# Chunked delta-rule attention before a Fourier-mixing MLP: chunks of 64 tokens instead of 128, triangular blocks inverted on VectorE instead of TensorE

## The chip, the cores and the metric

One core of one Trainium2 chip. The metric is the time of one execution in device microseconds (us); the median of several runs counts.

## The reference, cut to what matters

```python
B, H, S, D = 4, 8, 768, 48              # fp32 throughout
k_n = k / (norm(k) + 1e-6)
for t in range(S):                      # per batch and head, state is D x D
    y[t]  = q[t] @ state
    v_old = state.T @ k_n[t]
    state = state + beta[t] * outer(k_n[t], v[t] - v_old)
x   = y as (B, S, H*D = 384)
u   = x + real(fft(fft(x, axis=seq), axis=channel))
un  = (u - mean(u)) / sqrt(var(u) + 1e-6)
out = u + relu(un @ w_ch1) @ w_ch2      # 384 -> 1536 -> 384
```

## The kernel before, in words

The recurrence is done in chunks of C = 128 tokens, one chunk on the 128 partitions, all 8 heads side by side: 4 batches x 6 chunks = 24 steps. `load` (L132) brings a chunk of k, v and q with three DMAs on SP's queue (192 KB each, rows of 192 bytes), two steps ahead. `pre` (L239) does what needs no state: norms of k (L247 to L253), 12 transposes on TensorE (tile `pt`, L267, copied out by ScalarE, L268), the products k k' and k q' (tile `pg`, L281), and the inverse of each head's four 32 x 32 diagonal blocks. That inverse is five rounds of doubling (L306 to L336); a round is 32 small matmuls into `px` and 32 or 64 into `pn`, each on 32 x 32 of the array. The four blocks of a head lie on the four partition groups of 32, so four neighbours in the instruction stream use four different row groups and four different column groups of the array, and all write one PSUM tile of 2 KB a partition. VectorE masks `px` into `Y` (L314), ScalarE copies `pn` into `Tn` (L330, L333).

`seq` (L339) carries the state: subtract k times state (`pk`, L350), solve the four blocks of 32 rows in turn (`pa`, `pu`, L355 to L367), then the state's increment `pS` (L373) and the output `py` (L377, L379), which becomes a row block of `x` (L387).

`post` (L392) takes a finished batch: sums and differences for the real DFT (L402, L403 on POOL, L406 to L413 on VectorE), DFT along the sequence (`pf`) and along the channels (`pb`, L445) with the additions into x and the norm statistics (L451 to L459), then for each of three groups of 256 tokens the normalised rows are transposed (`ptr`), 72 matmuls make `ph` (1536 hidden channels, relu on VectorE and ScalarE in turn, L486, L488) and 48 make `po`, which is added to x and stored. The weights come as 64-bit floats and are turned into fp32 by VectorE and POOL (`weights`, L183): six pieces of 1.5 MB with ten VectorE instructions each, while batch 0's attention runs.

Each fp32 matmul shows as two MATMUL and two LDWEIGHTS records in the profile; a transpose shows as one.

The order of work is written by generators: in step n the loop at L516 advances `seq(n)`, `pre(n+1)` and a side generator (`weights` in batch 0, `post(b-1)` afterwards) in turn; the tile framework then orders instructions on each engine's queue, by and large in that order but moving ready ones ahead. Each engine works off its queue in order. The last `post` runs alone at the end.

Of the kernel before, what the change touches and what calls it, by code (L numbers as in the profile page):

```python
# [9 lines left out]
F32 = mybir.dt.float32  # L10
# [6 lines left out]
C = 128  # L17
W = 32
LEVELS = (1, 2, 4, 8, 16)


def _consts(S, DM):

    p = np.arange(128)
    c = np.arange(W)
    r = p % W
    ident = np.eye(128)
    su = (p[None, :] > p[:, None]).astype(np.float64)
    bd = su * (p[None, :] // W == p[:, None] // W)
    grp = (p[:, None] // W == np.arange(128 // W)[None, :]).astype(np.float64)  # L30
    eye_c = (r[:, None] == c[None, :]).astype(np.float64)
    lev = []
    for n in LEVELS:
        off = ((r[:, None] // n) % 2 == 1) & (c[None, :] // n == r[:, None] // n - 1)
        lev.append(eye_c - off)
    pack = np.concatenate([ident, su, bd, grp, eye_c] + lev, axis=1)
# [27 lines left out]
def kernel(  # L64
# [14 lines left out]
    NC = S // C  # L79
    NP = H // 2  # L80
    NG = 128 // W
# [14 lines left out]
    io = ctx.enter_context(tc.tile_pool(name="io", bufs=2))  # L96
# [3 lines left out]
    def ps_pre(shape, name):  # L100
        return ps.tile(shape, F32, tag="pre", bufs=3, name=name)

    def ps_seq(shape, name):
        return ps.tile(shape, F32, tag="seq", bufs=2, name=name)

    def ps_post(shape, name):
        return ps.tile(shape, F32, tag="post", bufs=3, name=name)
# [9 lines left out]
    NKQ = 2  # L117
    kqs = []
    for i in range(NKQ):
        t = const.tile([128, 3, H, 64], F32, name=f"kq{i}")  # L120
        nc.gpsimd.memset(t, 0.0)
        kqs.append(t)
    states = []
    for i in range(2):
        t = const.tile([128, NP, 2, D], F32, name=f"state{i}")
        nc.gpsimd.memset(t, 0.0)
        states.append(t)

    steps = [(b, c) for b in range(B) for c in range(NC)]
    loaded = {}  # L130

    def load(n):  # L132
        b, c = steps[n]
        kq = kqs[n % NKQ]
        K4 = io.tile([128, H, D], F32, tag="K4", name="K4")
        V4 = io.tile([128, H, D], F32, tag="V4", name="V4")
        rows = slice(c * C, (c + 1) * C)
        nc.sync.dma_start(out=K4, in_=k[b, :, rows, :].rearrange("h p d -> p h d"))
        nc.sync.dma_start(out=kq[:, 2, :, 0:D], in_=q[b, :, rows, :].rearrange("h p d -> p h d"))
        nc.sync.dma_start(out=V4, in_=v[b, :, rows, :].rearrange("h p d -> p h d"))  # L140
        loaded[n] = (K4, V4)

    pack = const.tile([128, 3 * 128 + NG + W * (1 + len(LEVELS))], F32, name="pack")
    nc.scalar.dma_start(out=pack, in_=cn["pack"].ap())
    bt = const.tile([NBH, S], F32, name="bt")
    nc.scalar.dma_start(out=bt, in_=beta.rearrange("b h s -> (b h) s"))
    load(0)

    ident = pack[:, 0:128]
    m_su = pack[:, 128:256]  # L150
    m_bd = pack[:, 256:384]
    o = 3 * 128
    m_grp = pack[:, o:o + NG]
    eye_c = pack[:, o + NG:o + NG + W]
    m_lev = [pack[:, o + NG + W * (i + 1):o + NG + W * (i + 2)] for i in range(len(LEVELS))]

# [9 lines left out]

    ident_b = const.tile([128, 128], BF16, name="ident_b")
    nc.vector.tensor_copy(ident_b, ident)
    eye_b = const.tile([128, H, W], BF16, name="eye_b")
    nc.vector.tensor_copy(eye_b, eye_c[:, None, :].broadcast_to([128, H, W]))  # L170
    half_p = const.tile([128, H], F32, name="half_p")
    nc.gpsimd.memset(half_p, 0.5)
    half_n = const.tile([128, GT], F32, name="half_n")
    nc.gpsimd.memset(half_n, -0.5)


    psb = ps_pre([128, NC, NBH], "psb")
    for c in range(NC):
        tr(psb[:, c, :], bt[:, c * C:(c + 1) * C], c == 0)
    bcol = const.tile([128, NC, B, H], F32, name="bcol")  # L180
    nc.vector.tensor_copy(bcol.rearrange("p c b h -> p c (b h)"), psb)
# [54 lines left out]
    ready = {}  # L236
    xs = {}

    def pre(n):  # L239

        b, c = steps[n]
        kq = kqs[n % NKQ]
        K4, V4 = loaded.pop(n)
        bc = bcol[:, c, b]

        Ksq = wk.tile([128, H, D], F32, tag="Ksq", name="Ksq")
        nc.gpsimd.tensor_tensor(Ksq, K4, K4, op=ALU.mult)  # L247
        nrm = wk.tile([128, H], F32, tag="nrm", bufs=2, name="nrm")
        nc.vector.tensor_reduce(nrm, Ksq, axis=AX.X, op=ALU.add)
        nc.gpsimd.tensor_tensor(nrm, nrm, half_p, op=ALU.pow)  # L250
        nc.vector.tensor_scalar(nrm, nrm, 1e-6, None, op0=ALU.add)
        nc.vector.reciprocal(nrm, nrm)
        nc.vector.tensor_tensor(kq[:, 0, :, 0:D], K4, nrm[:, :, None].broadcast_to([128, H, D]),  # L253
                                op=ALU.mult)
        nc.gpsimd.tensor_tensor(kq[:, 1, :, 0:D], kq[:, 0, :, 0:D],  # L255
                                bc[:, :, None].broadcast_to([128, H, D]), op=ALU.mult)
        Vb = wk.tile([128, H, D], F32, tag="Vb", bufs=2, name="Vb")
        nc.gpsimd.tensor_tensor(Vb, V4, bc[:, :, None].broadcast_to([128, H, D]), op=ALU.mult)
        yield

        K1T = wk.tile([128, NP, 128], F32, tag="K1T", name="K1T")
        KQT = wk.tile([128, 2, NP, 128], F32, tag="KQT", bufs=2, name="KQT")
        for a, dst in ((2, KQT[:, 1]), (0, K1T), (1, KQT[:, 0])):
            pt = ps_pre([128, NP, 128], "pt")
            src = kq[:, a].rearrange("p h d -> p (h d)")
            for j in range(NP):
                tr(pt[:, j, :], src[:, 128 * j:128 * j + 128], j == 0)  # L267
            nc.scalar.activation(dst, pt, ACT.Copy)  # L268
            yield


        AT = wk.tile([128, H, 128], F32, tag="AT", bufs=2, name="AT")
        LQ = wk.tile([128, H, 128], F32, tag="LQ", bufs=2, name="LQ")
        Abd = wk.tile([128, H, 128], F32, tag="Abd", name="Abd")
        hv = "p (j e) t -> p e j t"
        for a in range(2):
            pgs = [ps_pre([128, NP, 128], f"pg{e}") for e in range(2)]
            for j in range(NP):
                for e in range(2):
                    pr = slice(64 * e, 64 * e + D)  # L280
                    mm(pgs[e][:, j, :], K1T[pr, j, :], KQT[pr, a, j, :], j == 0)  # L281
            for e in range(2):
                pg = pgs[e]
                if a == 0:
                    nc.vector.tensor_tensor(Abd.rearrange(hv, e=2)[:, e], pg,
                                            m_bd[:, None, :].broadcast_to([128, NP, 128]),
                                            op=ALU.mult)
                    nc.scalar.activation(AT.rearrange(hv, e=2)[:, e], pg, ACT.Copy)
                else:
                    nc.vector.tensor_tensor(LQ.rearrange(hv, e=2)[:, e], pg,  # L290
                                            m_su[:, None, :].broadcast_to([128, NP, 128]),
                                            op=ALU.mult)
            yield
# [3 lines left out]


        def blocks(o, lhsT, rhs):
            for h in range(H):  # L300
                for g in range(NG):
                    rw = slice(W * g, W * g + W)
                    mm(o[rw, h, :], lhsT(h, g, rw), rhs(h, g, rw), False)

        T = TT = None
        for i in range(len(LEVELS)):  # L306
            last = i == len(LEVELS) - 1
            px = ps_pre([128, H, W], "px")
            mm(px, ident_b, eye_b, True, False)
            blocks(px, lambda h, g, rw: Abd[rw, h, rw],  # L310
                   (lambda h, g, rw: eye_c[rw]) if T is None else
                   (lambda h, g, rw: T[rw, h, :]))
            Y = wk.tile([128, H, W], F32, tag="Y", bufs=2, name="Y")
            nc.vector.tensor_tensor(Y, px, m_lev[i][:, None, :].broadcast_to([128, H, W]),  # L314
                                    op=ALU.mult)
            yield
            pn = ps_pre([128, 2, H, W], "pn")
            first = [True] * NG
            for a in ((1, 0) if i > 0 and not last else (0,)):
                for h in range(H):  # L320
                    for g in range(NG):
                        rw = slice(W * g, W * g + W)
                        left, right = (TT, Y) if a else (Y, TT)
                        r = eye_c[rw] if right is None else right[rw, h, :]
                        mm(pn[rw, a, h, :], left[rw, h, :], r, first[g])
                        first[g] = False
                yield
# [237 lines left out]
```

## Time and profile before

| what | value |
|---|---|
| median of 3 runs (lowest to highest) | 1342.58 us (1340.2 to 1362.03) |
| the profiled execution's own time | 1334.15 us |
| its span, first to last instruction | 1332.4 us |
| TensorE busy (matmul records) | 1179.3 us, 26758 matmul records |
| VectorE / ScalarE / POOL busy | 411.6 / 252.9 / 171.5 us |

PE is TensorE's matmul row, PEld its weight loads, DVE VectorE, ACT ScalarE, POOL GpSimd, SP the engine whose queue issues most DMAs. A row of the timeline merges neighbouring records of the same kind: its length goes from the first start to the last end. Records of pipelined matmuls overlap, so the pace of a row of n matmuls is its length less one matmul's own duration, divided by n - 1. The granted clock is given as a share of 2.4 GHz, so 0.50 is 1.2 GHz; the clock's own record begins 249 us into the span, and the views show 1.00 before that where nothing was recorded.

### The profile page before, as it was taken

The numbers are of one execution on the slowest core, as the hardware profiler recorded it, in microseconds if no ns is written. First come the engines' busy times: TensorE is split into PE (matmuls) and PEld (weight loads), VectorE is DVE, ScalarE is ACT, GpSimd is POOL, SyncE is SP. The second block draws the span as 40 slices with busy tenths as digits, with TensorE's granted clock in tenths as the row PEclk, the third lists the DMA queues.
The fourth block names the chain that finished last, engine by engine and source line by source line (L and its number), as shares of the span: only waits on it lengthen the run. The fifth ranks groups of instructions, "written<-read, shape, count | busy, mean of one in ns | idle before, by whom it ended". The sixth has DMA issues, their size and how long they took to land. (4 is left out here: it accounts for less than half of the span.)

```text
span 1332.4 us, 55673 instructions
## 1 busy us (share of the span) xinstructions
PE 1179.3 (89%) x26758; PEld 929.8 (70%) x26758; DVE 411.6 (31%) x843; ACT 252.9 (19%) x529; POOL 171.5 (13%) x160
## 2 busy tenths in 40 slices
PE   3688798897899999999889999989989998997998
PEld 2576686786777677676777676766866775766776
DVE  3756721222162132231252222322441221314111
ACT  1111011011132112111321221211321220212000
POOL 4422310120020010120021011110111000001000
PEclk9999999756699899999999999899999999997999
DMA  8321000000010000100010010010100000000000
GB/s 211 104 67 56 15 15 14 16 20 15 3 27 15 21 21 14 33 15 20 10 28 15 20 21 18 22 21 15 21 15 15 14 3 9 8 8 6 12 12 13
DMA packets 81156, 33.60 MB, mean 25 GB/s; under 512 B 75426, under 2 KB 78595, under 8 KB 80547
## 3 DMA queue, kind: packets, MB, share of 16 engines
q1 hardware_dynamic: 80352, 28.32, 8.6%
q8 instruction: 209, 3.42, 1.1%
q10 hardware_dynamic: 578, 1.73, 0.4%
q14 instruction: 17, 0.13, 0.0%
HBM read 25.32 MB, written 4.72 MB: 23 GB/s over the span
## 5 line engine op out<-in xcount | busy, mean ns | idle before, releaser
L110 PE MATMUL ph<-unT,w 128*128 128x256 f32 x864 | 223.0, 397 | 4.8 <-issue 2.9
L110 PE MATMUL po<-w,hT 128*128 128x384 f32 x576 | 208.1, 502 | 0.0
L110 PEld LDWEIGHTS ph<-unT,w 128*128 128x128 f32 x864 | 157.0, 194 | 25.9 <-ACT unT L477 2.8
L110 PEld LDWEIGHTS po<-w,hT 128*128 128x128 f32 x576 | 103.8, 191 | 58.1
L314 DVE TENSOR_TENSOR Y<-px,pack 128x256 f32<-128x256 f32 x120 | 50.6, 422 | 271.6 <-PE px L110 271.5
L110 PE MATMUL pn<-Tn,Y 32*32 32x32 f32 x6144 | 87.4, 206 | 38.1 <-issue 34.1
L110 PEld LDWEIGHTS pn<-Tn,Y 32*32 32x32 f32 x6144 | 74.5, 117 | 56.1 <-issue 46.4
L110 PEld LDWEIGHTS px<-Tn,Abd 32*32 32x32 f32 x4608 | 55.1, 117 | 67.8 <-issue 40.0
L333 ACT ACTIVATE Tn<-pn 128x512 f32<-128x512 f32 x72 | 43.0, 597 | 306.4 <-PE pn L110 306.4
L110 PE MATMUL px<-Tn,Abd 32*32 32x32 f32 x4608 | 66.6, 206 | 36.5 <-issue 28.1
L110 PE MATMUL pg<-KQT,K1T 48*128 48x128 f32 x768 | 89.6, 334 | 2.4 <-ACT KQT L268 2.1
L110 PEld LDWEIGHTS pu<-R,Tn 32*32 32x32 f32 x1280 | 70.1, 119 | 26.6 <-issue 18.6
L110 PE MATMUL pn<-Y,Tn 32*32 32x32 f32 x4608 | 62.6, 205 | 27.5 <-DVE Y L314 24.0
L110 PEld LDWEIGHTS pn<-Y,Tn 32*32 32x32 f32 x4608 | 53.2, 117 | 47.7 <-DVE Y L314 25.7
L361 DVE TENSOR_TENSOR R<-R,pa 32x384 f32<-32x384 f32 x60 | 33.2, 553 | 165.9 <-PE pa L110 165.8
L110 PE MATMUL pu<-R,Tn 32*32 32x48 f32 x1280 | 82.0, 221 | 0.8 <-issue 0.8
L366 ACT ACTIVATE U<-pu 32x384 f32<-32x384 f32 x96 | 46.3, 482 | 187.7 <-PE pu L110 187.3
L110 PEld LDWEIGHTS pg<-KQT,K1T 48*128 48x128 f32 x768 | 73.5, 226 | 10.2 <-ACT KQT L268 3.3
L110 PEld LDWEIGHTS pa<-U,AT 64*32 64x32 f32 (+2 forms) x1152 | 63.3, 122 | 24.4 <-issue 19.8
L255 POOL TENSOR_TENSOR kq<-kq,bcol 128x384 f32<-128x384 f32 x24 | 21.9, 914 | 448.2 <-DVE kq L253 412.0
L110 PE MATMUL pa<-U,AT 64*32 64x48 f32 (+2 forms) x1152 | 74.1, 224 | 0.0
L113 PE MATMUL pt<-pack,kq 128*128 128x128 f32 x288 | 57.9, 335 | 17.6 <-DVE kq L253 9.0
(98 smaller groups left out, 1300.8 us busy)
## 6 DMA issues: line engine op xcount, KB each, us to landing
w<-in_moe_w_ch_dram SPq DMA_DIRECT2D x6, 1536.0 KB, 8.0
K<-in_k_dram SPq DMA_DIRECT2D x24, 192.0 KB, 2.8
V<-in_v_dram SPq DMA_DIRECT2D x24, 192.0 KB, 2.8
kq<-in_q_dram SPq DMA_DIRECT2D x24, 192.0 KB, 2.9
out_dram<-x SPq DMA_DIRECT2D x24, 192.0 KB, 1.9
evt<-k_even ACTq DMA_DIRECT2D x1, 579.0 KB, 6.0
odt<-k_odd ACTq DMA_DIRECT2D x1, 576.0 KB, 7.3
pack<-k_pack ACTq DMA_DIRECT2D x1, 290.0 KB, 3.2
```

The lines of the kernel that those rows point to most:

```text
L110: nc.tensor.matmul(o, lhsT=lhsT, rhs=rhs, start=start, stop=stop, skip_group_check=True)
L113: nc.tensor.matmul(o, lhsT=src, rhs=ident[0:src.shape[0], 0:src.shape[0]], is_transpose=True, start=start, stop=True, skip_group_check=True)
L255: nc.gpsimd.tensor_tensor(kq[:, 1, :, 0:D], kq[:, 0, :, 0:D], bc[:, :, None].broadcast_to([128, H, D]), op=ALU.mult)
L314: nc.vector.tensor_tensor(Y, px, m_lev[i][:, None, :].broadcast_to([128, H, W]), op=ALU.mult)
L333: nc.scalar.activation(Tn, pn, ACT.Copy)
L361: nc.vector.tensor_tensor(R[rw], R[rw], pa[rw], op=ALU.subtract)
L366: nc.scalar.activation(U[rw], pu[rw], ACT.Copy)
```

## The change

What is computed stays. The attention part is written anew; `weights` and the Fourier and MLP code stay, cut into two generators (`fourier`, `mlp`).

- Chunks of C = 64 tokens. A load still covers L = 128 tokens (two chunks). Heads 0 to 3 lie on partitions 0 to 63, heads 4 to 7 on 64 to 127. So there are 24 loads and 48 chunk steps.
- Work that needs no state runs a load or more ahead: `pre_a(g)` (4 transposes of k, the 32 x 32 and 32 x 64 blocks of k k' on array tiles of 64 x 32), `invert(r)` for a round of RL = 4 loads, `pre_b(g)`.
- `invert` puts one 32 x 32 block on each (partition, column) place: two DVE transposes turn the 128 x 1024 tile so that each partition holds one whole block, the norms of k are taken from the blocks' diagonals (ScalarE Sqrt and two Newton steps on VectorE), and forward substitution is 31 steps of one multiply and one add on VectorE over (31-j)(j+1) elements a partition, j = 0 to 30. POOL zeroes the result tile.
- `pre_b` transposes q, joins the two 32-blocks of a 64-chunk (`px`, `py`), masks k q' (`LQ`, VectorE), and multiplies the inverse M by K and by V (`WT`, `U0`) on 64 x 64 tiles of the array.
- `step(g, c)` is then: 8 matmuls `pw` (WT times state), one VectorE subtraction, 8 matmuls `pk`, one VectorE addition into the new state; after the second chunk 32 matmuls and a ScalarE and a VectorE instruction make the output rows of x.
- PSUM: pairs of banks (`pair`, 2 buffers), single ones (`one`, 2), and `post` with 2 buffers where there were 3.
- k, q and v come with four DMAs of 48 KB each per load instead of one of 192 KB, k up to seven loads ahead. beta comes with 32 small DMAs per round of four loads on POOL's queue, where it was one DMA and six transposes at the start.
- The loop: `pre_a` of four loads, `invert(0)` and `pre_b(0)` stand ahead of it. In step n it advances `step`, then parts of `pre_a`, `invert` or `pre_b`, then the side generator (`weights` in batch 0, `mlp(b-1)` afterwards, four pieces a step, nine pieces kept back). After a batch's last step `fourier(b)` runs beside the pieces kept back.

```diff
-C = 128
+C = 64
+L = 128
 W = 32
-LEVELS = (1, 2, 4, 8, 16)
+RL = 4
+RING = 7
...
+    def fetch(dst, src, g):
+        b, n = divmod(g, NL)
+        for hh in range(2):
+            for c in range(2):
+                t0 = n * L + c * C
+                nc.sync.dma_start(out=dst[hh * C:hh * C + C, c],
+                                  in_=src[b, 4 * hh:4 * hh + 4, t0:t0 + C, :].rearrange(
+                                      "j t d -> t j d"))
...
+    def pre_a(g):
+        K = Ks[g % RING]
...
+        for i in range(4):
+            c, jj = divmod(i, 2)
+            tr(pt[:, 128 * i:128 * i + 128],
+               K[:, c, 2 * jj:2 * jj + 2, :].rearrange("p j d -> p (j d)"), i == 0)
+        nc.scalar.activation(KT.rearrange("p c j t -> p (c j t)"), pt, ACT.Copy)
+        yield
...
+        for i in range(4):
+            c, jj = divmod(i, 2)
+            for q4 in range(4):
+                for jp in range(2):
...
+                    mm(pg[q4 * W:q4 * W + W, jp, C * i:C * i + C],
+                       KT[lo[jp], c, jj, t0 + blk * W:t0 + blk * W + W], rhs, i == 0)
...
+    def invert(r):
...
+        nc.gpsimd.memset(M, 0.0)
+        nc.vector.transpose(A, G.rearrange("p m s -> p s m"))
+        yield
...
+        nc.scalar.activation(nrm, diag, ACT.Sqrt)
...
+        nc.vector.scalar_tensor_tensor(A, A, -1.0, bn[:, :, None].broadcast_to([128, W, W]),
+                                       op0=ALU.mult, op1=ALU.mult)
...
+        for j in range(W - 1):
+            n = W - 1 - j
...
+            nc.vector.tensor_tensor(t, A[:, j + 1:W, j:j + 1].broadcast_to([128, n, j + 1]),
+                                    M[:, j:j + 1, 0:j + 1].broadcast_to([128, n, j + 1]),
+                                    op=ALU.mult)
+            nc.vector.tensor_tensor(M[:, j + 1:W, 0:j + 1], M[:, j + 1:W, 0:j + 1], t, op=ALU.add)
+            yield
+
+        nc.vector.transpose(A.rearrange("p m t -> p t m"), M)
+        nc.vector.transpose(G.rearrange("p m s -> p s m"), M.rearrange("p t s -> p s t"))
...
+    def pre_b(g):
...
+        for c in range(2):
+            for j in range(4):
+                for hh in range(2):
+                    mt = MT[full[hh], 4 * c + j].rearrange("p b t -> p (b t)")
+                    jj, jp = divmod(j, 2)
+                    o = (2 * c + jj) * C
+                    mm(pw[full[jp], hh, o:o + C], K[full[hh], c, j, :], mt, c == 0 and jj == 0)
+                    o = (4 * c + j) * D
+                    mm(pu[full[hh], o:o + D], mt, V[full[hh], c, j, :], c == 0 and j == 0)
...
+    def step(g, c):
...
+            pw = ps_pair()
+            for jj in range(2):
+                for hh in range(2):
+                    for jp in range(2):
+                        mm(pw[full[hh], jp, D * jj:D * jj + D], WT[lo[jp], hh, c, jj, :],
+                           s0[lo[jp], hh, jj, :], jj == 0)
+            nc.vector.tensor_tensor(
+                U.rearrange("p (jj jp) e -> p jp jj e", jp=2),
+                U.rearrange("p (jj jp) e -> p jp jj e", jp=2),
+                pw[:, :, 0:2 * D].rearrange("p a (j e) -> p a j e", e=D), op=ALU.subtract)
+            yield
...
+    for g in range(RL):
+        drain(pre_a(g))
...
+    drain(invert(0))
+    load_qv(1)
+    drain(pre_b(0))
     side = weights()
...
+    for n in range(2 * NLT):
...
+        live = [(step(g, c), 1)]
...
+            if ri in (0, 1, 2):
+                live.append((pre_a(nxt + ri), 1))
+            elif ri == 3:
+                live.append((pre_a(nxt + 3), 1))
+                inv = invert(r + 1)
+            elif ri < 7:
+                live.append((part(inv, 12), 3))
...
+            want = (PIECES - KEEP) * (i + 1) // (2 * NL)
+            live.append((part(side, want - done), 2))
...
+        run(live)
+        if i == 2 * NL - 1:
+            if b == 0:
+                drain(side)
+            f = fourier(b)
+            run([(f, 1)] + ([(side, 1)] if b > 0 else []))
+            side, done = mlp(b), 0
+    drain(side)
```

## Rows read from the trace of the kernel before

**Rows 1.** The page: busy time of each engine.

```profile
PE 1179.3 (89%) x26758; PEld 929.8 (70%) x26758; DVE 411.6 (31%) x843; ACT 252.9 (19%) x529; POOL 171.5 (13%) x160
```

**Rows 2.** Stages: length; PE, PEld, DVE, ACT, POOL busy (count); clock; DMA share, GB/s.

```profile
0.00:60.00 60.00, 25.04 (x859) 20.68 (x863) 34.21 (x45) 6.44 (x10) 23.74 (x23) 1.00 0.54 147
60.00:244.00 184.00, 157.15 (x3495) 136.71 (x3491) 82.53 (x110) 29.39 (x57) 39.28 (x19) 1.00 0.15 41
...
885.00:1204.00 319.00, 295.27 (x7136) 224.03 (x7136) 82.16 (x188) 66.46 (x140) 20.62 (x24) 0.98 0.05 13
```

**Rows 3.** Timeline, last `post`: start us, length us, engine, line, kind, count.

```profile
1204.46 0.99 POOL L402 TENSOR_TENSOR E<-x 128x384 f32<-128x384 f32 x1 [45.79 <-ACT x L387]
...
1229.55 18.58 PE L110 MATMUL ph<-unT,w 128*128 128x256 f32 x72 [0.58 <-ACT unT L477]
...
1297.54 15.81 PE L110 MATMUL ph<-unT,w 128*128 128x256 f32 x72 [0.69 <-ACT unT L477]
...
1313.18 15.64 PE L110 MATMUL po<-w,hT 128*128 128x384 f32 x48
```

**Rows 4.** Timeline: small matmuls between large ones.

```profile
1108.01 0.75 PE L110 MATMUL px<-Y,Abd 32*32 32x32 f32 x64
...
1108.69 2.85 PE L110 MATMUL po<-w,hT 128*128 128x384 f32 x8
...
1111.47 0.75 PE L110 MATMUL pn<-Y,Tn 32*32 32x32 f32 x64
```

**Rows 5.** Timeline: the attention's other matmul shapes, TensorE alone.

```profile
612.77 1.16 PE L110 MATMUL pg<-KQT,K1T 48*128 48x128 f32 x16
...
1101.84 0.67 PE L110 MATMUL pS<-U,kq 128*64 128x48 f32 x16
...
1132.29 0.66 PE L113 MATMUL pt<-pack,kq 128*128 128x128 f32 x4
1132.90 0.86 PE L110 MATMUL pu<-R,Tn 32*32 32x48 f32 x16
```

**Rows 6.** Transposes `pt` in two stretches: duration ns least/median/most, first and last start.

```profile
L113 PE MATMUL pt<-pack,kq x24: 421/421/475, 60.5 to 118.8; 128*128 128x128 f32 x24
...
L113 PE MATMUL pt<-pack,kq x36: 272/273/329, 602.6 to 697.6; 128*128 128x128 f32 x36
```

**Rows 7.** Groups by line, VectorE: busy us, mean ns of one, idle before.

```profile
L217 DVE TENSOR_SCALAR wlow<-w 128x1536 int32<-128x1536 int32 x6 | 14.7, 2454 | 0.0
L253 DVE TENSOR_TENSOR kq<-K,nrm 128x384 f32<-128x384 f32 x24 | 13.3, 553 | 46.1 <-PE pS L110 40.8 <-PE pt L113 5.2
L454 DVE TENSOR_TENSOR x<-x,Q 128x191 f32<-128x191 f32 x24 | 8.4, 348 | 0.0
L229 DVE TENSOR_SCALAR wlow<-w 128x1536 int32<-128x1536 int32 x6 | 6.3, 1056 | 0.0
```

**Rows 8.** Weights' tile `wtmp` by stage: length, DVE, POOL busy, clock, DMA; sums.

```profile
0.00:60.00 60.00, 17.56 (x16) 3.42 (x1) 1.00 0.54 147
...
sum 244.00, DVE 55.16 POOL 22.09; mean DVE 27.58 POOL 11.05
```

**Rows 9.** Timeline of the start: DMA issues on SP's queue, and three early instructions.

```profile
0.72 0.43 SPq L138 DMA_DIRECT2D K<-in_k_dram  x1
...
9.09 4.64 SPq L140 DMA_DIRECT2D V<-in_v_dram  x1
...
18.55 0.83 POOL L258 TENSOR_TENSOR Vb<-V,bcol 128x384 f32<-128x384 f32 x1 [8.15 <-DMA V<-in_v_dram]
...
24.45 0.78 DVE L251 TENSOR_SCALAR nrm<-nrm 128x8 f32<-128x8 f32 x1 [1.53 <-POOL nrm L250]
...
25.27 0.20 DVE L252 RECIPROCAL nrm<-nrm 128x8 f32<-128x8 f32 x1
```

**Rows 10.** Busy time by stage again, around the clock's first records.

```profile
246.00:263.00 17.00, 12.61 (x551) 10.16 (x551) 5.00 (x12) 1.79 (x3) 3.81 (x4) 0.68 0.08 15
263.00:311.00 48.00, 42.10 (x1022) 36.29 (x1021) 13.61 (x29) 7.57 (x15) 9.59 (x9) 0.61 0.09 19
```

More of the change, by code (lines that the diff above doesn't have):

```diff
@@ L132, in load @@
[L132 to L141, printed above, removed]
@@ L143 @@
[L143 removed]
+    Ks, Qs = [], []
+    for i in range(RING):
+        t = const.tile([128, 2, 4, 64], F32, name=f"K{i}")
+        nc.gpsimd.memset(t[:, :, :, D:64], 0.0)
+        Ks.append(t)
+    for i in range(2):
+        t = const.tile([128, 2, 4, 64], F32, name=f"Q{i}")
+        nc.gpsimd.memset(t[:, :, :, D:64], 0.0)
+        Qs.append(t)
+    NLT = B * NL
+    Vs = {}
+    def fetch(dst, src, g):
[6 more added lines that the diff above has]
+                                      "j t d -> t j d"))
@@ new lines, in load_k, with load_qv, load_beta @@
+    def load_k(g):
+        if g < NLT:
+            fetch(Ks[g % RING][:, :, :, 0:D], k, g)
+    def load_qv(g):
+        if g < NLT:
+            fetch(Qs[g % 2][:, :, :, 0:D], q, g)
+            Vs[g] = wk.tile([128, 2, 4, D], F32, tag="V", bufs=2, name="V")
+            fetch(Vs[g], v, g)
+    betas = {}
+    def load_beta(r):
+        if r * RL >= NLT:
+            return
+        t = wk.tile([128, W], F32, tag="beta", bufs=2, name="beta")
+        for i in range(RL):
+            b, n = divmod(RL * r + i, NL)
+            for q4 in range(4):
+                hh, blk = divmod(q4, 2)
+                p0 = q4 * W + i * 8
+                for c in range(2):
+                    t0 = n * L + c * C + blk * W
+                    nc.gpsimd.dma_start(out=t[p0 + 4 * c:p0 + 4 * c + 4],
+                                        in_=beta[b, 4 * hh:4 * hh + 4, t0:t0 + W])
+        betas[r] = t
@@ L144 @@
+    pack = const.tile([128, 128 + C + 2], F32, name="pack")
     nc.scalar.dma_start(out=pack, in_=cn["pack"].ap())
-    bt = const.tile([NBH, S], F32, name="bt")
-    nc.scalar.dma_start(out=bt, in_=beta.rearrange("b h s -> (b h) s"))
-    load(0)
+    for g in range(RL):
+        load_k(g)
+    load_beta(0)
+    load_qv(0)
     ident = pack[:, 0:128]
[L150 to L154, printed above, removed]
@@ L234, in weights @@
             yield
[L236 to L250, printed above, removed]
+    lo = [slice(64 * e, 64 * e + D) for e in range(2)]
@@ L299, in blocks @@
[L299 to L327, printed above, removed]
-            Tn = wk.tile([128, 2, H, W], F32, tag="Tn", bufs=3, name="Tn")
-            if i == 0 or last:
-                nc.scalar.activation(Tn[:, 0], pn[:, 0], ACT.Copy)
-                T = Y
-            else:
-                nc.scalar.activation(Tn, pn, ACT.Copy)
-                T = Tn[:, 1]
-            TT = Tn[:, 0]
-            yield
@@ L510, in advance @@
         return True
-    load(1)
-    for _ in pre(0):
-        pass
-    side = weights()
-    for n, (b, c) in enumerate(steps):
-        if n + 2 < len(steps):
-            load(n + 2)
-        if c == 0 and b > 0:
-            side = post(b - 1)
-        live = [seq(n)]
-        if n + 1 < len(steps):
-            live.append(pre(n + 1))
-        share = UNITS
-        while live or share:
-            live = [g for g in live if advance(g)]
-            if share:
-                share -= 1
-                advance(side)
-        if c == NC - 1:
-            for _ in side:
-                pass
@@ L533, with drain, run, part @@
-    for _ in post(B - 1):
-        pass
+    def drain(gen):
+        for _ in gen:
+            pass
+    def run(live):
+        while live:
+            live = [(g, n) for g, n in live if advance(g, n)]
+    def part(gen, n):
+        for _ in range(n):
+            if next(gen, "end") == "end":
+                return
+            yield
+    for g in range(RL):
+        drain(pre_a(g))
+    for g in range(RL, RING):
+        load_k(g)
+    load_beta(1)
+    drain(invert(0))
+    load_qv(1)
```

337 lines of the change are left out of this document (206 added, 131 removed).

## Prediction

> **What bounds the kernel now.** I read the page first: TensorE is busy for 89% of the span, no other engine above 31% [rows 1]. Then the stages. From 0 to 244 us batch 0's attention runs beside the weights' conversion; each of the next three stretches, of some 320 us, holds one batch's attention and the `post` of the batch before, with TensorE busy for 295 of 319 us in the last of them [rows 2]; the last 128 us are a `post` alone [rows 3]. So after 244 us the sum of TensorE's work decides, and the question is how much of it is attention.
>
> A `post` alone gives the rest. Its Fourier part lasts from 1204.46 to 1229.55, 25 us; then come three groups of `ph` and `po`, 15.8 + 15.6 us each at the full clock, 95 us in all [rows 3]. A stretch of 319 us is thus 95 + 25 of `post` and about 199 of attention, 33 us for each of 6 chunks of 128.
>
> Why 33? By the pace of each shape (a row's length less one matmul's own time, over its count less one): 32 x 32 tiles, four at a time, (0.75 - 0.20)/63 = 8.7 ns a record [rows 4]; `pu`, one tile at a time, (0.86 - 0.20)/15 = 44 ns; `pS`, two column halves, 30 ns; `pg`, two row halves of 128 columns, 59 ns; a transpose 0.13 us [rows 5]. The 1041 records of a chunk come to about 21 us. The rest is changing over: eight `po` matmuls between two small groups take 2.78 us from start to start (1108.69 to 1111.47) where 15.64/48 x 8 = 2.6 would do, and 64 small ones 0.68 where 63 x 8.7 ns is 0.55 [rows 3, 4], so about 0.33 us per small group between large ones. With about 29 groups a chunk that is 10 us; 21 + 10 = 31, close to the 33.
>
> **TensorE's new work, per load of 128 tokens.** The diff gives 8 transposes and 176 matmuls, so 360 records instead of 1041.
> - 8 transposes x 0.13 = 1.0 us.
> - `pg`, 64 records on eight tiles of 64 x 32: at the pace of four small tiles 0.56 us (far end 64 x 44 ns = 2.8).
> - `px` and `py`, 64 records two at a time: twice 8.7 ns, 1.1 us.
> - k q' (32), and `step`'s `pw`, `pk`, state and output products (128), on four 64 x 64 tiles. No row shows four such tiles at once. `pS` shows two column halves at 30 ns a record, `pg` two row halves together [rows 5]; both at once is 15 ns, 2.4 us (far end, one at a time like a single `pg` half scaled to 64 columns, 58 ns: 9.3 us).
> - M K and M V, 64 records whose order loads two of the four tiles more: 22 ns, 1.4 us (between 15 and 58 ns).
> Together 6.5 us. Groups between large work: 13 (two in `pre_a`, five in `pre_b`, six in the two steps) x 0.33 = 4.3 us. That is 10.8; I take 11, as the same sum fell short of 33 by 2 before. So 22 us less per load.
>
> `px`, `py` and the M V products write from two row groups into one PSUM buffer. So did `pn`, from four, at 8.7 ns a record [rows 4]. The Trainium skill (TensorEngine Tiling (Array Packing), Restrictions and Gotchas) says that different row tiles cannot use the same PSUM bank at a time; by that rule 96 records would go one by one at 44 ns, 4.2 us instead of 1.8, and 18 loads would cost 43 us more. The row speaks against it as long as the column groups differ, as they do here too; I take nothing for it.
>
> **VectorE's new work.** From 553 ns for 384 elements and 348 for 191, an instruction costs 0.147 us and 1.06 ns an element [rows 7]. One round's 31 steps are 62 instructions over 2 x 5456 = 10,912 elements: 9.1 + 11.6 us, and since each waits for the one before, 0.04 us between (24.45 + 0.78 to 25.27) [rows 9]: 23.2 us. Three transposes and the scaling of 1024 elements, no transpose being in the trace, I take as 1.2 us each; 13 small instructions 3 us. Some 30 us a round (far ends 20 and 40), 6 rounds 180. From round 1 on it lies beside TensorE: a round is spread over eight steps of about 15 us. Each hop of a step (`pw` to VectorE to `pk` to VectorE) takes 1 us with its queue, and between two of them the loop puts `pre` work and two pieces of `mlp` (1.3 to 2.6 us each on TensorE). Cost taken 0; if that cover fails, it is rival B. ScalarE gets about 5 us a load and perhaps two reloads of its function table a round for Sqrt, which no row here prices; even at the 2.45 us of the slowest VectorE row [rows 7] 12 would be 29 us on an engine that was busy for 19% [rows 1]: also 0. SP issues twelve DMAs a load for three, 12 x 0.43 = 5 us of some 30 a load [rows 9]; they are due a load or more later, so 0, and nothing but the stores of the output stands behind them.
>
> **The start.** k's four loads: six loads had landed at 18.55 us, 3 us each [rows 9], so 12 us; the last `pre_a` 5 us more, 17. Round 0 is wholly exposed: 30 us and a Sqrt hop of 2, to 49. POOL issues 32 DMAs for beta; a free issue on SP took 0.43 us, a blocked one 4.64 [rows 9]: 14 us (in time) to 148 (124 us late). I take near the low end and add 5. `pre_b(0)` is a chain of TensorE and ScalarE hops at the low clock, 9 us. First step at 63 us.
>
> **Batch 0.** VectorE holds weights, 55.2 us for `wtmp` [rows 8] and 14.7 + 6.3 for `wlow` [rows 7], 76; round 1, 30; steps and masks 6 x 2.7 = 16: 122 us, of which 9 fit in before. TensorE runs at the low clock here as before (transposes last 421 ns to 118.8 us and 273 later [rows 6]): 6 x 16, and some for later rounds, 100 us. With 8% lost, 123 us: batch 0 ends at 186 us instead of 244.
>
> **The sum.** Fourier part of batch 0: 26, to 212 us. Three stretches of 95 (MLP) + 6 x 11 (attention) + 20 (Fourier part: 15 of TensorE, 5 of gaps, as the nine pieces kept back run beside it) = 181 each, to 755. The last MLP 97. Span 852 us; the profiled execution was 1.75 us above its span, 854, and the median of the runs 0.6% above the profiled one: 859, rounded to **860 us** (the case's own range 800 to 930).
>
> **Rivals.**
> A, quicker (0.15). Waits and groups are fewer than counted, because the tile framework moves ready work ahead: 8 us a load, and batch 0 hides its VectorE work better by 20. For it: VectorE had done 17.6 us of the weights' work by 60 us [rows 8], before the loop's first step. Against: the 29 groups of before had the same freedom. 860 - 18 x 3 - 20 = 786 us.
> B, VectorE in front of TensorE (0.20). Rounds 1 to 5 are waited for, 5 x 28 us less little cover, or each load's eight hops are exposed by 1 us: 18 x 8 = 144. Either way some 140: 1000 us. For it: `post` has one PSUM buffer less, and relu on VectorE stands behind six chained instructions of the inversion. Against: VectorE was busy for 82 of 319 us [rows 2]; even with all of that kept and 56 us of rounds and steps added it is 138 in 181.
> C, 64 x 64 tiles one at a time (0.07). 224 records x 58 ns = 13 us instead of 3.8, 166 us over 18 loads and 60 in batch 0: 1086 us. Against: both kinds of halves overlapped in rows 5.
> D, the clock (0.03), the one that ends slower. From 263 to 311 us the granted clock was 0.61, though TensorE was busy for 42 of 48 us; before it, from 246, it was busy for 12.6 of 17 [rows 10]. If the new mix is held at 1.2 GHz to the end, each MLP costs 190, attention 17.5 a load, the Fourier part 35: 63 + 123 + 30 + 3 x 330 + 194 = 1400. It outweighs the gain from 88% of the time after batch 0 on. Against: the clock was 0.98 from 885 to 1204 [rows 2], when the large matmuls were 30% of the stretch; now they are half. The Trainium skill (TensorE: Matmul & The Clock Gate, Part 1) says that the low clock is the default and that activity lifts it; by that rule more large matmuls make D less likely, and the rows after 400 us agree with it, those around 300 us only in part.
> That the change does not do what it says, the inversion landing on TensorE's path, is B.
>
> **How the numbers follow.** Forecast 0.55, A 0.15, B 0.20, C 0.07, D 0.03. The range 785 to 1000 us takes in A and B and the moderate end of a late beta, and leaves out C, D and 1 in 10 of the rest. Faster by over 2% (about what a measurement here can tell from no change) needs less than 1316 us: the forecast, A, B and C, 0.97; D split between same, 0.01, and slower, 0.02.
>
> **What would show it.** Right: about 10,500 matmul records; TensorE still the busiest; first `pw` near 63 us; `pw`, `pk` records at about 15 ns; 62 chained VectorE instructions in 21 to 26 us a round; stretches between the Fourier parts near 180 us; clock at 0.95 or more after batch 0. Wrong: TensorE waiting on VectorE by over 100 us in total (B), `pk` at 58 ns (C), a granted clock near 0.5 past 250 us (D), the first beta landing after 30 us.

## The result, and the profile after

The changed kernel takes 893.3 us (median of 4 runs, 892.9 to 894.9) where the kernel before took 1341.4 beside it: a ratio of 0.669, with a 95% interval of 0.663 to 0.675. Ratios, and the times of the experiments, leave out executions in a slower state that programs fall into at times (here the 1362.0 of the kernel before and an 871.5 below), so 0.669 is not 893.3/1341.4. The forecast was 860 and its range 785 to 1000. The profiled execution has a span of 891.1 us, 39 above the forecast's 852. That difference hides two larger errors of opposite sign, as the trace shows.

The page's busy time of each engine, of the changed kernel, against [rows 1]:

```profile
PE 689.5 (77%) x10344; PEld 528.7 (59%) x10344; DVE 431.1 (48%) x1028; ACT 180.1 (20%) x440; POOL 217.6 (24%) x314
```

TensorE's work fell from 1179 to 690 us, the span by 441. Busy time by stage, of the changed kernel (columns as in [rows 2]):

```profile
24.00:146.00 122.00, 1.44 (x34) 0.94 (x32) 95.11 (x143) 2.48 (x5) 64.39 (x70) 1.00 0.29 88
160.00:257.00 97.00, 64.56 (x2040) 55.27 (x2035) 50.29 (x126) 27.14 (x63) 31.37 (x49) 0.67 0.22 37
257.00:300.00 43.00, 38.92 (x363) 33.81 (x353) 31.91 (x101) 11.43 (x33) 22.97 (x42) 0.76 0.13 21
300.00:440.00 140.00, 130.43 (x2106) 98.34 (x2104) 75.51 (x187) 33.78 (x83) 35.84 (x52) 0.96 0.15 28
600.00:790.00 190.00, 184.39 (x2182) 139.34 (x2183) 87.25 (x242) 40.80 (x104) 18.60 (x24) 1.00 0.07 16
790.00:891.00 101.00, 95.54 (x368) 69.24 (x366) 11.93 (x27) 8.86 (x22) 0.92 (x2) 0.99 0.03 12
```

The first row is the surprise: for 122 us TensorE does 1.4 us of work while VectorE does 95. From 300 us on TensorE is busy 93 to 97% of the time, at 0.96 to 1.00 of the full clock. The low clock of [rows 10] is there again, 0.67 and 0.76 up to 300 us, and no longer: rival D is out. Waits of TensorE, of the changed kernel (waiting for what; us in total, times, longest):

```profile
PE one L104 <- DVE G L321: 140.3, 5, 119.9
PE pf L104 <- DVE E L490: 9.4, 2, 6.8
```

One wait of 119.9 us, for the last transpose of `invert(0)` (L321), holds the whole gap. Timeline of VectorE inside it, where round 0's 31 steps (L314, L317) should run as one chain:

```profile
43.67 0.96 DVE L213 TENSOR_SCALAR wtmp<-w 128x1536 int32<-128x1536 int32 x1 [11.59 <-DMA w<-in_moe_w_ch_dram]
...
45.41 0.19 DVE L308 COPY M<-bn 128x32 f32<-128x32 f32 x1
...
61.19 0.95 DVE L215 TENSOR_SCALAR wtmp<-wtmp 128x1536 int32<-128x1536 int32 x1
62.06 0.33 DVE L314 TENSOR_TENSOR tmp<-A,M 128x175 f32<-128x175 f32 x1
62.31 1.75 DVE L218 SCALAR_TENSOR_TENSOR wtmp<-wlow,wtmp 128x1536 f32<-128x1536 int32 x1
63.98 0.33 DVE L317 TENSOR_TENSOR M<-M,tmp 128x175 f32<-128x175 f32 x1
...
73.24 0.40 DVE L317 TENSOR_TENSOR M<-M,tmp 128x231 f32<-128x231 f32 x1
80.94 0.96 DVE L213 TENSOR_SCALAR wtmp<-w 128x1536 int32<-128x1536 int32 x1 [7.31 <-POOL w L232]
```

Nearly every instruction of the chain has one of the weights' conversion (`wtmp`, three to five times as long) in front of it, though `weights` is written behind `invert(0)` in the program. The last two rows add a second price: the chain's next instruction stands behind a `wtmp` instruction that waits 7.3 us for POOL. The first two show the same at the chain's head: its first instruction on M stands behind a `wtmp` that waits 11.6 us for the weights' DMA, although POOL's zeroing of M had ended at 38.8. In these rows the chain needs 0.33 us an instruction and gets one per 1 to 2 us.

VectorE by groups, of the changed kernel (busy us, mean ns of one, idle before), against [rows 7]:

```profile
L317 DVE TENSOR_TENSOR M<-M,tmp 128x31 f32<-128x31 f32 (+15 forms) x186 | 68.7, 369 | 4.0
L314 DVE TENSOR_TENSOR tmp<-A,M 128x31 f32<-128x31 f32 (+15 forms) x186 | 68.2, 367 | 4.1
L321 DVE STREAM_TRANSPOSE G<-M 128x1024 f32<-128x1024 f32 x6 | 11.9, 1986 | 0.0
L286 DVE STREAM_TRANSPOSE A<-G 128x1024 f32<-128x1024 f32 x6 | 11.7, 1946 | 26.9 <-ACT G L274 26.9
L306 DVE SCALAR_TENSOR_TENSOR A<-A,bn 128x1024 f32<-128x1024 f32 x6 | 7.4, 1226 | 0.2
```

The steps are (68.7 + 68.2)/6 = 22.8 us a round (worked out: 20.7 and gaps); a transpose of 1024 elements is 1.95 us (taken as 1.2), the scaling 1.23 (1.2). Timeline of TensorE in batches 2 and 3, of the changed kernel, against [rows 4, 5]:

```profile
464.75 0.69 PE L104 MATMUL pair<-QT,KT 48*64 48x64 f32 x32
465.38 0.69 PE L104 MATMUL one<-A,XM 32*32 32x32 f32 x32
466.00 2.86 PE L104 MATMUL ph<-unT,w 128*128 128x256 f32 x12
...
741.44 0.45 PE L104 MATMUL pair<-U,K 64*64 64x48 f32 x16
741.82 1.56 PE L104 MATMUL ph<-unT,w 128*128 128x256 f32 x6
...
745.11 0.45 PE L104 MATMUL pair<-S,WT 48*64 48x48 f32 x16
745.49 2.86 PE L104 MATMUL ph<-unT,w 128*128 128x256 f32 x12
748.28 0.68 PE L104 MATMUL pair<-S,QT 48*64 48x48 f32 x32
```

`pair<-U,K` is `pk`. A single record of a 64 x 48 tile lasts 0.20 to 0.25 us; with 0.24 its pace is (0.45 - 0.24)/15 = 14 ns a record, so the 64 x 64 tiles overlap and rival C is out. From its start to the next row's start it takes 0.38 us, so the change-over costs the small group about 0.38 - 16 x 0.014 = 0.16 us. The large work pays too: from 745.49 to 748.28 are 2.79 us for 12 records of `ph`, which alone take 12 x 15.64/72 = 2.61 [rows 3], another 0.18. Together that is 0.34, the 0.33 assumed. But large work gives way to a small group only 67 times in the last two batches, some 6 times a load, by count in the timeline. Start to start at the full clock, all small groups of a load come to 8.1 us: `pw` and `pk` 0.38 each, twice; M K with M V 1.55; `LQ` U 0.79; k q' 0.6; the blocks of k k' 0.79; `px`, `py` 0.62 each; state products 0.5; the transposes 0.54 and 0.59.

So the span divides like this (first `pw`, and the start of the last E sum on POOL, which is the end of batch 0):

| | forecast | changed kernel | weights and later rounds left out (below) |
|---|---|---|---|
| first `pw` | 63 | 158.7 | 73.6 |
| batch 0 after it | 123 | 98.2 | 71.9 |
| the rest | 666 | 634.2 | 613.1 |
| span | 852 | 891.1 | 758.6 |

The two rows that divide it, of the changed kernel:

```profile
158.66 0.45 PE L104 MATMUL pair<-S,WT 48*64 48x48 f32 x16
256.94 1.00 POOL L482 TENSOR_TENSOR E<-x 128x384 f32<-128x384 f32 x1 [9.23 <-DVE x L465]
```

### The profile page after: what moved, and what is told of

Its sections match the earlier page's. It is cut to its first block, busy times and chain, and to the rows that moved or that the text cites. A ratio compares the mean times of both kernels' runs of the same rounds, so it can differ in the third digit from the quotient of the medians.

```text
span 891.1 us, 23482 instructions
## 1 busy us (share of the span) xinstructions
PE 689.5 (77%) x10344; PEld 528.7 (59%) x10344; DVE 431.1 (48%) x1028; ACT 180.1 (20%) x440; POOL 217.6 (24%) x314
## 5 line engine op out<-in xcount | busy, mean ns | idle before, releaser
L104 PE MATMUL one<-G,GX 32*32 32x32 f32 x768 | 18.0, 199 | 140.3 <-DVE G L321 140.3
L157 POOL DMA_DIRECT2D beta<-in_beta_dram x192 | 104.8, 554 | 8.5 <-DMA beta<-in_beta_dram 3.6
L573 DVE TENSOR_SCALAR hT<-ph 128x256 f32<-128x256 f32 x72 | 30.3, 421 | 123.7 <-PE ph L104 123.7
L317 DVE TENSOR_TENSOR M<-M,tmp 128x31 f32<-128x31 f32 (+15 forms) x186 | 68.7, 369 | 4.0
L314 DVE TENSOR_TENSOR tmp<-A,M 128x31 f32<-128x31 f32 (+15 forms) x186 | 68.2, 367 | 4.1
L571 ACT ACTIVATE hT<-ph 128x256 f32<-128x256 f32 x72 | 27.6, 383 | 135.8 <-PE ph L104 135.7
L104 PE MATMUL pair<-MT,K 64*64 64x64 f32 x768 | 45.6, 258 | 2.9 <-ACT MT L380 1.2
L104 PE MATMUL one<-V,MT 64*64 64x48 f32 x768 | 46.9, 236 | 0.0
L104 PEld LDWEIGHTS pair<-MT,K 64*64 64x64 f32 x768 | 40.6, 149 | 6.4 <-issue 3.9
L104 PEld LDWEIGHTS one<-V,MT 64*64 64x64 f32 x768 | 42.9, 155 | 0.3 <-issue 0.2
L232 POOL TENSOR_TENSOR w<-wtmp 128x1536 f32<-128x1536 f32 x6 | 25.3, 4216 | 56.7 <-DVE wtmp L231 56.7
```

What stands on the lines that cost most here:

```text
L104: nc.tensor.matmul(o, lhsT=lhsT, rhs=rhs, start=start, stop=stop, skip_group_check=True)
L157: nc.gpsimd.dma_start(out=t[p0 + 4 * c:p0 + 4 * c + 4], in_=beta[b, 4 * hh:4 * hh + 4, t0:t0 + W])
L232: nc.gpsimd.tensor_tensor(dst.rearrange("p c f -> p (c f)"), man.bitcast(F32), exp.bitcast(F32), op=ALU.mult)
L314: nc.vector.tensor_tensor(t, A[:, j + 1:W, j:j + 1].broadcast_to([128, n, j + 1]), M[:, j:j + 1, 0:j + 1].broadcast_to([128, n, j + 1]), o ...
L317: nc.vector.tensor_tensor(M[:, j + 1:W, 0:j + 1], M[:, j + 1:W, 0:j + 1], t, op=ALU.add)
L571: nc.scalar.activation(hT[:, fc, :], ph, ACT.Relu)
```

## The experiments

The theory after the result: VectorE's queue, worked off in order, sets the time up to the end of batch 0. The rivals were that VectorE's work costs the same wherever it stands, and that TensorE at its low clock holds batch 0.

**The weights behind round 0, then beta too.** The weights' ten VectorE instructions a piece are queued behind round 0's last transpose; in the second kernel also the 32 beta DMAs of round 1 behind the `memset` of M on POOL.

```diff
+    def behind():
+        return tc.issue_after(anchor[0])
...
+            with behind():
                 nc.vector.tensor_scalar(man, hi, 3, 0x007FFFF8, ...
...
-        nc.vector.transpose(G.rearrange("p m s -> p s m"), M.rearrange("p t s -> p s t"))
+        fin = nc.vector.transpose(G.rearrange("p m s -> p s m"), M.rearrange("p t s -> p s t"))
+        anchor.setdefault(0, fin.ins)
```

> The changed kernel with one ordering edge: the weights' VectorE instructions are queued behind the last transpose of round 0's inversion. Theory 1 (the weights' instructions stretch the exposed round 0, and their own time does not come back because batch 0 is bound by TensorE and hops, not by VectorE): round 0's 31 steps shrink from 97 us (46 to 143) to about 26, the first pw comes at 80 us instead of 159, batch 0 then lasts 115 to 125 instead of 98, and the time falls by 50 to 60 us to 835 to 845. Rival (VectorE's total up to the end of batch 0 is what counts, in whatever order): batch 0 grows by all of the 75 us of weights, and the time stays within 10 us of 893.

> As the run before, and POOL issues round 1's 32 beta DMAs behind the zeroing of round 0's tile instead of ahead of it. Theory 1: the zeroing ended at 38.8 us because 16 us of DMA issues stood ahead of it on POOL; VectorE then waits no more and the first pw comes 6 to 7 us earlier than in the run before, the time 5 to 7 us lower. Rival (the wait is for something else, such as the first beta): no difference beyond 2 us.

Measured: 865.8 us, ratio 0.649 (0.646 to 0.652), and 869.5, ratio 0.652 (0.650 to 0.655). First `pw` came at 80.5 and 73.8, as expected, so the order in VectorE's queue is the cause of the gap, beta's 7 us aside. Of the 78 us won there only 28 arrived, between the 50 to 60 of the theory and the 10 at most of the rival: batch 0 now lasted 154 and 159 us. Stages of the second kernel:

```profile
0.00:74.00 74.00, 22.24 (x634) 17.38 (x636) 46.23 (x95) 13.43 (x29) 55.59 (x107) 1.00 0.45 108
74.00:233.00 159.00, 71.59 (x2069) 61.68 (x2061) 105.02 (x178) 27.93 (x65) 77.71 (x66) 0.56 0.24 59
```

The weights moved into batch 0 and stand between round 1's instructions there (from 107 us to the start of its last transpose at 195, for some 33 us of work). Beta's 7 us were gained at the first `pw` and down to 2 by the end of the batch; the time did not fall, where 5 to 7 us had been expected.

**Without the later rounds' steps; without the weights; without both.** Three kernels, run once each, that bound the two costs: the 31 steps of the rounds 1 to 5 left out of the changed kernel; the weights' VectorE instructions, and POOL's product with them, left out of the changed kernel with beta behind the `memset`; and both.

```diff
         for j in range(W - 1):
+            if r > 0:
+                yield
+                continue
...
+            nc.gpsimd.memset(dst, 0.01)
```

> The changed kernel without the 31 steps of forward substitution in rounds 1 to 5 (left out: those blocks keep only their diagonal); round 0 is whole. Theory 1 (those 5 x 25 us of VectorE lie beside TensorE's work): the time falls by no more than 15 us, all of it in batch 0 where little else runs. Rival B of the prediction (TensorE waits for the rounds): it falls by 60 to 140 us.

> The changed kernel with the weights' ten VectorE instructions a piece left out (the weights are loaded as before but set to a constant by POOL), and with POOL's order of the second run. Theory 1 (prediction's terms): round 0 ends near 62 us, the first pw comes near 73, batch 0 lasts about 98 us as in the changed kernel, and the time is 800 to 815; so against the second run the weights cost 20 to 30 us. Rival (the start is bound by the loads or the beta DMAs, not by VectorE): the first pw stays past 100 us.

> Leaves out both: the weights' ten VectorE instructions (POOL writes 0.01 into w1 and w2, as in the run without the weights) and the 31 steps of the rounds 1 to 5. Theory (it is one sum, VectorE's, in front of everything until about 285 us, in which the weights and the rounds 1 and 2 stand): with the weights gone only some of round 1 and 2 is still waited for, 23 + 12 at most of it, so 813 becomes 785 to 800. Rival (weights and rounds are two separate waits, each with its own place): the 44 us of the run without steps come off in full: 770.

Measured: 849.2, 813.3 and 760.6 us. The steps cost 44 us in the changed kernel (15 at most by the theory, 60 or more by the rival) and 53 with the weights gone, of 114 us of work; the weights 56 once out of round 0 (20 to 30 expected), of some 70. So neither lies beside TensorE, as the forecast had it; the 44 came off in full and more, as the rival said. The stages of the last one show the kernel with most of VectorE's early work out of the way:

```profile
74.00:146.00 72.00, 62.13 (x2051) 53.19 (x2048) 29.62 (x65) 27.56 (x65) 43.87 (x72) 0.76 0.37 74
146.00:300.00 154.00, 145.96 (x2391) 113.51 (x2383) 68.75 (x162) 40.77 (x102) 56.79 (x92) 0.97 0.16 30
300.00:600.00 300.00, 294.55 (x4490) 223.99 (x4482) 101.42 (x247) 77.84 (x193) 31.32 (x39) 1.00 0.12 25
```

TensorE is busy for 86% of batch 0 and 95 to 98% after it. Against this kernel the weights' and the steps' work, with POOL's products and the beta order that differ too, costs the changed kernel 132 us: 85 before the first `pw`, 26 in batch 0, 21 later.

**The weights behind round 1; round 1 pulled forward.** The same, with `anchor[1]` and the weights traced from step 7 on; then also `pre_a` of loads 4 to 6 ahead of the loop and `invert(1)` at steps 3 to 5.

```diff
-        return tc.issue_after(anchor[0])
+        return tc.issue_after(anchor[1])
...
+    for g in range(RL, RING):
+        drain(pre_a(g))
```

> As the last order (weights behind round 0, second round's beta transfers behind the memset), but the ten VectorE instructions of the weights stand behind the last transpose of round 1 instead of round 0, traced from step 7 on, six pieces a step. Theory (VectorE's queue in order is what holds batch 0: its fifth and sixth load need round 1's inverse, and batch 0 ends about 36 us after that): first pw stays near 74, round 1 ends near 140 (as where the weights were left out) instead of 195, batch 0 ends near 175 instead of 233; the weights then run from 140 to 215 and delay the first MLP, so that of the 56 us that they cost only some 25 to 35 come back: 830 to 840 us. Rival (the sum of VectorE's work up to the first MLP counts, whatever its order, because attention of batch 1 finds nothing to do beside): 860 to 870 us, with batch 0 ending at 175 all the same.

> As the kernel with the weights behind round 1, and round 1 itself is pulled forward: the products pre_a of the loads 4 to 6 ahead of the loop, that of load 7 at step 2, round 1's inversion at steps 3 to 5, the weights from step 6, five pieces a step. Theory: round 1 starts as soon as VectorE is through with round 0 and load 7's product (near 85 instead of 106), ends at 115 to 125, batch 0 ends at 150 to 165, the weights are done near 190 to 200, and the time is 800 to 825 us, below 830 to 840 of the kernel without the pull. Rival (the first MLP waits for the weights, and these for VectorE's sum, so that an earlier round 1 only moves a wait): batch 0 ends earlier by 10 to 25, but the time differs from the other kernel's by less than 8 us.

Measured: 867.7 us, ratio 0.649 (0.643 to 0.655), and 859.6, ratio 0.645 (0.641 to 0.649). A miss against the 830 to 840 and 800 to 825 expected: round 1's last transpose started at 134 and 128 us, and batch 0 ended still at 212 and 207. That batch 0 had ended 36 us after round 1 in the runs so far was no cause. The timeline of VectorE of the first of the two shows what holds it now:

```profile
179.41 0.34 DVE L429 TENSOR_TENSOR U<-U,pair 128x192 f32<-128x192 f32 x1
179.68 4.14 DVE L225 TENSOR_SCALAR wlow<-w 128x1536 int32<-128x1536 int32 x1
183.74 0.34 DVE L448 TENSOR_TENSOR S<-S,pair 128x192 f32<-128x192 f32 x1
184.00 0.95 DVE L220 TENSOR_SCALAR wtmp<-w 128x1536 int32<-128x1536 int32 x1
...
190.88 0.95 DVE L237 TENSOR_SCALAR wtmp<-wtmp 128x1536 int32<-128x1536 int32 x1
191.75 0.68 DVE L381 TENSOR_TENSOR LQ<-pair,pack 128x512 f32<-128x512 f32 x1
192.35 1.74 DVE L242 TENSOR_TENSOR wtmp<-wtmp,wlow 128x1536 int32<-128x1536 int32 x1
194.02 0.34 DVE L429 TENSOR_TENSOR U<-U,pair 128x192 f32<-128x192 f32 x1
```

U, S, `LQ`, U: each of attention's short instructions waits behind a run of the weights' (from one U to the next 14.6 us), and TensorE behind them. What stands in front has changed, not the place.

**Added matmuls in batch 0.** Four matmuls in each of batch 0's twelve chunk steps that nothing reads (48, twice what the expectation counts), to see whether TensorE's low clock sets batch 0.

```diff
+                pd = ps_post([128, 2 * NE], "pd")
+                mm(pd, ident, evt[:, 0, :], True)
```

> The changed kernel, with added matmuls that nothing reads: four of 128 rows by 386 columns, fp32, to each of batch 0's six steps into a free PSUM buffer (24 in all; about 0.65 us a quarter-speed pass each, some 16 to 32 us of TensorE's time). They answer whether TensorE (its low granted clock of 181 to 229, or its sum) or VectorE's queue sets the end of batch 0. Theory (round 1's end gates): batch 0 ends within 8 us of 256.9, the time within 10 us of the changed kernel's 893. Rival (TensorE at its low clock is the bound of batch 0): the added work lengthens batch 0 by 15 to 30 us, or, where it lifts the clock, shortens it by as much.

Measured: 893.7 us, batch 0's end at 259. Inconclusive for its question: all had started by 58 us, long before batch 0's steps, as the tile's rows show (duration ns least, median, most, first and last start):

```profile
L104 PE MATMUL pd<-evt,pack x96: 485/487/1012, 10.1 to 57.7; 128*128 128x386 f32 x96
```

Waiting for nothing, they were moved ahead, most of them into the gap, as the weights had been. What the low clock itself costs batch 0 stays open.

**Half of the weights in batch 1; the first piece earlier; the second half behind round 2.** From the kernel with round 1 forward: w2's three pieces traced beside batch 1; then w1's first piece behind round 0 instead of round 1; then w2 behind `invert(2)`, the MLP's second half from step 5 of batch 1.

```diff
-    side = weights()
+    side, w2side = weights(0), weights(1)
...
-        return tc.issue_after(anchor[1])
+        return tc.issue_after(anchor[(0, 1, 1, 2, 2, 2)[i]])
...
+            if b == 1 and i in (4, 5):
+                live.append((part(w2side, 8), 8))
```

> As the kernel with round 1 pulled forward, but only the three pieces of the first matrix (w1) stand behind round 1; the three of the second (w2) are traced beside the first three steps of batch 1, after the Fourier part of batch 0, and the MLP needs them first at its second half. Theory (in batch 0 each VectorE operation of attention stands behind a whole piece of the weights, some 15 us a piece, so batch 0's end is pushed by what stands ahead of it on VectorE): batch 0 ends near 165 to 175 instead of 207; TensorE then has the Fourier part and batch 1's attention to do while VectorE converts w2; 825 to 845 us against 860. Rival (VectorE's sum up to the end of batch 1 counts, with round 2's inversion and the MLP's evictions in it): batch 0 ends 30 us earlier, but the end of batch 1 moves by less than 8: 853 to 862.

> As the kernel with w2 in batch 1, and the first piece of w1 stands behind round 0 instead of round 1, in the 15 us in which VectorE waits for the first loads' TensorE products. Theory: first pw stays within 4 of 78, round 1 ends within 8 of 128, batch 0 ends 5 to 12 us earlier than with three pieces behind round 1, the time 3 to 12 us below it. Rival (the transfer of the first piece lands only near 68 and its ten instructions then stand ahead of pre_b and round 1): round 1 ends 10 to 15 later and nothing is gained.

> As the best order so far (w1's first piece behind round 0, the others behind round 1, w2 in batch 1), but w2's three pieces stand behind the end of round 2, traced at steps 4 and 5 of batch 1; the MLP of batch 0 does its first half group before, its w2 products from step 5 on. Theory (VectorE's order counts as long as TensorE waits for round 2; the longest wait of the run before is 35 us for that round's last transpose): round 2 ends near 235 to 245 instead of 278, w2 is done near 285, TensorE takes batch 1's attention meanwhile, and 851 becomes 825 to 842. Rival (the MLP that is put off fills no gap later, since TensorE is full after 285 us): within 8 us of 851, batch 1 ending earlier but the rest of the MLP standing behind it.

Measured: 861.5 us, ratio 0.648 (0.643 to 0.654): no gain, and the rival's number. Then 850.7, ratio 0.639 (0.635 to 0.643), 11 us less where 3 to 12 were expected, with intervals that just touch. Then 823.1, ratio 0.617 (0.612 to 0.622), below the expected 825. The last two differ in where w2 and the MLP's second half of batch 0 stand. VectorE in round 2, first of the one with w2 beside it:

```profile
229.71 0.39 DVE L328 TENSOR_TENSOR tmp<-A,M 128x231 f32<-128x231 f32 x1
230.02 1.75 DVE L228 SCALAR_TENSOR_TENSOR wtmp<-wlow,wtmp 128x1536 f32<-128x1536 int32 x1
231.69 0.39 DVE L331 TENSOR_TENSOR M<-M,tmp 128x231 f32<-128x231 f32 x1
```

and then of the one with w2 behind it:

```profile
233.29 0.19 DVE L331 TENSOR_TENSOR M<-M,tmp 128x31 f32<-128x31 f32 x1
233.52 1.90 DVE L334 STREAM_TRANSPOSE A<-M 128x1024 f32<-128x1024 f32 x1
235.29 1.97 DVE L335 STREAM_TRANSPOSE G<-M 128x1024 f32<-128x1024 f32 x1
237.15 2.09 DVE L222 TENSOR_SCALAR wtmp<-w 128x1536 int32<-128x1536 int32 x1
```

Round 2 ends at 278 us in the first and 235 in the second (start of the last transpose), batch 1 at 377 and 351, the span at 848 and 821. The work is the same; the chain went first. The 35 us that the expectation gives as TensorE's wait for round 2 are its wait for round 0. For round 2 it is short in both. Waits of TensorE for that transpose, in the first from 181 to 285 us:

```profile
PE one L104 <- DVE G L335: 1.4, 1, 1.4
```

and in the second from 177 to 285 us:

```profile
PE one L104 <- DVE G L335: 6.3, 1, 6.3
```

What changed is how much TensorE had to do meanwhile: from 181 to 285 us it was busy for 77 us with 742 records in the first and for 90 with 1443 in the second, which had batch 1's blocks 43 us earlier. That is half of the 27 us; the other half is not accounted for. This version beats both kernels: 8% below the changed one, by the ratios to the kernel before.

**M K and M V not ahead.** One part of the change undone: `pre_b` of a load is traced as a whole ahead of its own first step.

```diff
+        if c == 0 and n > 0:
+            drain(pre_b(g))
```

> The changed kernel with one part undone: pre_b (M K, M V and what leads to them) of a load is traced as a whole ahead of that load's own first step, not a load ahead in parts beside the steps. Theory (after 300 us TensorE is full of other work, and the framework moves ready work ahead of the chain): 893 becomes 895 to 925, most of it in batch 0, where nothing fills in. Rival (the chain px, ScalarE, py, ScalarE, M K, ScalarE of about 6 us a load is exposed at all loads but the first): 23 x 6 = 138, 1030 us.

Measured: 891.1 us, ratio 0.668 (0.663 to 0.674), against 0.669 (0.663 to 0.675): no difference. The rival's 138 us are excluded, and so is most of the theory's 2 to 32. Where the program writes `pre_b` within a load makes no difference here; that the framework's moving of ready work does it fits the runs above, but only the result is shown.

## Why the prediction was right or wrong

The time was inside the range and 4% above the forecast. That it came so near is luck: errors of +143 and -104 us nearly cancel (last point). By its steps:

- **The start, "first step at 63 us": wrong by 96.** With the weights out of the way it is 73.8, 11 too early, of which 7 before round 0 (its first transpose starts at 24 us, not 17) and 5 in it (37 us to the end of its last transpose, not 32). Of the other 85, 7 are round 1's beta DMAs, issued ahead of the zeroing of M on POOL; 78 came from the sentence that took the weights to fit beside: [rows 8] showed them moved ahead of the loop's first step, and rival A used that as a gain. In a kernel whose start waits for a VectorE chain it is a loss. The table of [rows 8] was read, and its sign not. The timeline of the kernel before has it in small too: from 50.96 to 54.43 us four `wtmp` instructions in a row stand in front of a `Y` (L314) for which TensorE waits 2.73 us.
- **Batch 0, 123 us: 98.2,** only because the weights had been done before. With the weights in it, as the forecast had them, it lasted 154 and 159 us, and VectorE was busy for 105 of the 159: the loss taken as 8% was 34%. The sum over VectorE's work (weights 76, some 70 measured; a round 30) was about right as work, not in place: the end of batch 0 came at 257 instead of 186.
- **"From round 1 on it lies beside TensorE; cost taken 0": wrong.** The steps alone cost 44 us, 26 of it by the end of batch 0 and 12 in batch 1. This was rival B's mechanism (1000 us, five rounds of 28). It holds for rounds 1 and 2, where [rows 2]'s idle share of VectorE says nothing of when a round's chain gets its turn; after 300 us the last transpose of a round is waited for only 4.6 us in total. The sign that the prediction set for B, over 100 us of waits on VectorE, did show (140.3 us for `G` above), but 119.9 of them are round 0 behind the weights, not B's rounds.
- **TensorE's 11 us a load: some 9.** The matmuls' paces were about right (15 ns for `pk`, 14 measured; 1.4 us for M K and M V, 1.55 with its change-over), and so was the 0.33 us per change-over (0.16 + 0.18 above). Too large was the number of groups between large work: 13 a load were counted and some 6 found, because small groups stand next to each other; 8.1 + 6 x 0.18 = 9.2. 18 x 1.8 = 32 of the 53 us by which the rest, 666, is shorter with VectorE out of the way, 613. In that kernel some 500 of the 6336 records of these 18 loads had also run by the end of batch 0, and MLP and Fourier parts took some 9 us less than the 468 in the sum. Here rival A, fewer groups and 8 us, was the better one. The two row groups writing one buffer cost nothing that shows: `py` above, 32 records in 0.69 us, is (0.69 - 0.20)/31 = 16 ns a record with 0.20 for a single one, so the restriction cited from the Trainium skill (TensorEngine Tiling (Array Packing), Restrictions and Gotchas), which would have them one by one, does not show in this trace either.
- **Inversion, 30 us a round: near enough as work:** 22.8 for the steps, 1.2 for the scaling, 5.9 for transposes that were sized at 3.6, and some 3 of small ones, 33.
- **Rivals.** C and D fell to the rows above. A and B each held a part, with opposite signs: +85 and about +47 from VectorE, +11 from the start, -53 from the rest (666 to 613), and batch 0 without weights and steps 72 where 123 with them stood, -51. Together +39, the 39 measured.

## What to carry over

A long chain of short dependent instructions that another engine waits for must be protected in its engine's queue: bulk work that is ready goes between its links, and each link then costs a bulk instruction (25 us of steps became 96 in round 0). A sum of busy time per engine does not show that; ask, for each wait that sets the end, what else is ready on the engine waited for, and queue it behind the chain. What is queued there can stand in front of other short instructions next: the first such move brought 28 of the 78 us that it won. The same instructions in another order were worth 70 us here, 893 to 823.

## What the runs showed of the hardware

VectorE's transpose of 128 x 1024 fp32 takes 1.95 us, 1.9 ns an element, where its products run at 1.06 [rows 7]. Some VectorE instructions that usually take 0.3 to 0.95 us took 3.4 to 4.15 while POOL multiplied a piece of the weights (`L225` above, 4.14 against 0.95 elsewhere; POOL's own multiply ran from 179.57 for 3.43 us beside it). That the two engines hold each other up there is suggested by the times and was not tried alone. Beta's 192 DMAs cost POOL 104.8 us of issue, 0.55 each. A small group of array tiles between large matmuls costs 0.16 us of TensorE's time on its own side and 0.18 on that of the large matmuls, beyond what both take alone.
